# Projection matmuls of an attention and gated-MLP kernel issued as four 32-column tiles

## The chip, the cores and the metric

The kernel runs on one core of a Trainium2 chip. The time is device microseconds of one execution, given as a median over runs; beside it stands one profiled execution, with the span from its first to its last instruction. Engine names: PE is the matrix engine (PEld are its weight loads), DVE the vector engine, ACT the scalar engine, POOL the GpSimd engine, SP the engine that issues most DMAs.

## What is computed

The input x is layer-normalised, and two branches read the result: multi-head attention with 32 heads of 20 columns, and a gated MLP. They are multiplied after a SiLU and added to x.

```python
x = A_x                                   # 1 x 2048 x 640, bf16
xn = _layernorm(x, axis=-1)
# attention: H = 32, Dh = 20
qkv = (xn @ wqkv).reshape(B, S, 3, H, Dh)
scores = einsum("bhqd,bhkd->bhqk", q, k) * Dh ** -0.5
o = einsum("bhqk,bhkd->bhqd", softmax(scores), v)
s = o @ wo
# gated MLP: F = 1728
h = sigmoid(xn @ w_gate) * (xn @ w_up)
g = silu(h @ w_down)
return x + s * g
```

## The kernel before

**Stages.** A first stage normalises 16 token tiles of 128 rows, transposes them into `xnT` (128 model rows x 5 slices x 2048 tokens, in four chunks of 512 tokens), and computes K, the first Q and part of V for the first four heads. Then the main stage runs 32 blocks: 8 groups of four heads (`GH`) times 4 chunks of 512 queries (`QC`). A last stage finishes the final block's output rows.

**The score path.** A score tile is 128 keys x 512 queries of one head. It has a contraction of 32 rows (20 used, one for a bound), so the four heads of a group stand in four row quarters of the PE array: `score_mm` (L859-861) uses `tile_position=(32*j, 0)`. The array form is "rows". A round writes up to two score tiles into one of two double banks `scA`, and up to two more into the three single banks `bk` (`bank`).

**Two engines take exponentials.** ACT reads `scA` (a pair at once), sometimes with a third tile in a `bk` (L1171, L1172), and writes `pt`. DVE takes other tiles from a `bk` by integer steps: an `iv` pass per tile (L1194) and three passes over four tiles (L945, L948, L951) that make `pb`. Every score tile goes to one of the two engines: ACT's is one PV matmul, DVE's two.

**The PV path.** `pv_emit` (L887-901) multiplies with V. The stationary operand has 21 columns, and the four heads stand in four column quarters, `tile_position=(0, 32*j)`, all adding into one bank `oacc`. The array form is "columns", four matmuls in a round.

**The projections.** K and Q for the first two groups (`k_mm1` L467, `mk_q` L471), K and Q for units of six heads (120 columns, `u_mm` L503), gate and up for 128 hidden columns each (`mk_gu` L622, `mm` and `mm2`): each is 5 matmuls, one for each slice of the contraction, of a 128 x 128 (or 120) weight against 512 tokens of `xnT`, into one `bk`. `q_bound` (L173) adds one more to a Q. These use the whole array ("none"). V (`mk_v`), the down projection (`mk_down`) and the output projection (`mk_out`) hold tokens stationary and also use the whole array. In the first stage `k_mm` and `q_mm` (L138, L163) do the same work as whole-array matmuls.

**The order.** The order on PE, ACT and DVE is written out by a planner at build time: it steps a clock `now` by 0.02 us, gives each operation a fixed duration, and emits the instruction that it picks. On PE it chooses between a score round ("F"), a PV round ("PV") and the next matmul of a projection item ("M"). `T_F`, `T_PV` and `T_MM` are 0.2133; a step in another `mode` than the one before pays `T_MODE`, 0.107. An item takes a `bk` that is free (`flex`), and releases it when DVE or ACT has read it. DVE claims a score tile in a round if its queue is short and a bank is free (L1283, L1288); what it does not claim goes to ACT. SP's DMAs (gate and up weights, Q and K through DRAM, the softmax divisor) are issued in the order in which the planner reaches them.

Of the kernel before, what the change touches and what calls it, by code (L numbers as in the profile page):

```python
# [18 lines left out]
P = 128  # L19
# [9 lines left out]
UC = UH * DH  # L29
# [20 lines left out]
def kernel(  # L50
# [11 lines left out]
    nc = tc.nc  # L62
# [4 lines left out]
    KD = D // P  # L67
# [30 lines left out]
    xnT = persist.tile([P, NQC, KD, QC], BF16, name="xnT")  # L98
# [13 lines left out]
    mds = [const.tile([P, P], BF16, name=f"md{i}") for i in range(2)]  # L112
# [16 lines left out]
    def wslice(g, t, kd):  # L129
        return wqks[g % 2][:, kd * 2 + t, :, :].rearrange("p j e -> p (j e)")  # L130
# [37 lines left out]
    def q_abs(ps):  # L168
        aq = wk.tile([P, QC], BF16, tag="aq", bufs=4, name="aq")
        nc.scalar.activation(out=aq, in_=ps, func=ACT.Abs)  # L170
        return aq

    def q_bound(ps, g, aq):  # L173
        nc.tensor.matmul(ps, lhsT=mds[g % 2], rhs=aq, start=False, stop=True, skip_group_check=True)

    def q_evac(ps, q):
        nc.vector.tensor_scalar_mul(out=q, in0=ps, scalar1=qscale)
# [218 lines left out]
    wgu_tiles = {}  # L396
# [23 lines left out]
    T_F, T_PV, T_MM, T_MODE = 0.2133, 0.2133, 0.2133, 0.107  # L420
# [44 lines left out]
            ev_at[("md", g)] = t + 0.3  # L465

    def k_mm1(ps, g, c, kd):  # L467
        nc.tensor.matmul(ps, lhsT=wslice(g, 1, kd), rhs=xnT[:, c, kd, :],
                         start=(kd == 0), stop=(kd == KD - 1))

    def mk_q(b, at):  # L471
        g, c = divmod(b, NQC)
        st = {}

        def alloc():
            st["ps"] = misc_ps()

        def mm(kd):
            nc.tensor.matmul(st["ps"], lhsT=wslice(g, 0, kd), rhs=xnT[:, c, kd, :],
                             start=(kd == 0), stop=(kd == KD - 1))  # L480

        def ab():
            st["aq"] = q_abs(st["ps"])

        def ev():
            q_evac(st["ps"], qts[b % 3])
        return Item([("PE", alloc, [(T_MM, lambda kd=kd: mm(kd)) for kd in range(KD)]),
                     ("ACT", 0.48, ab),
                     ("PE", None, [(T_MM, lambda: q_bound(st["ps"], g, st["aq"]))]),
                     ("DVE", 0.60, ev, "free", lambda t: q_at.__setitem__(b, t))], at, pre=[("md", g)])  # L490


    wus, mku = {}, {}
# [7 lines left out]
        wus[u] = w  # L501

    def u_mm(st, u, i, c, kd):  # L503
        nc.tensor.matmul(st["ps"][0:UC, :], lhsT=wus[u][:, kd, i, :], rhs=xnT[:, c, kd, :],  # L504
                         start=(kd == 0), stop=(kd == KD - 1))

    def mk_ku(u, c, at):
        st = {}
# [113 lines left out]
    def mk_gu(c, kf, at):  # L622
# [15 lines left out]

        def mm(key, i, kd):
            w = wgu_tiles[(c, k2)]  # L640
            nc.tensor.matmul(st[key][0:fs, :], lhsT=w[:, i, kd, ko * P:ko * P + fs],  # L641
                             rhs=xnT[:, c, kd, :], start=(kd == 0), stop=(kd == KD - 1))

        def th():
            st["t"] = w2.tile([P, QC], BF16, tag="tnh", bufs=2, name="tnh")
# [4 lines left out]
                                           in1=st["u"][0:fs, :], op0=ALU.add, op1=ALU.mult)  # L650

        def mm2(kd):
            nc.tensor.matmul(st["g"], lhsT=wgu_tiles[(c, k2)][:, 0, kd, P:2 * P],
                             rhs=xnT[:, c, kd, :], start=(kd == 0), stop=(kd == KD - 1))

        def th2():
            st["t"] = w2.tile([P, QC], BF16, tag="tnh", bufs=2, name="tnh")
# [380 lines left out]
    with tc.manual_schedule(engines={ENG.PE, ENG.Activation, ENG.DVE}):  # L1038
# [16 lines left out]
        dve_pass = []  # L1055
        dve_last = None
        cur = None
        mode = None
        blk_loaded = -1
        active = []  # L1060
        u_next, k_next, q_next, k_at = 0, PG, PG * NQC, {}
# [37 lines left out]
        while chain or items or glu_items or any(it.i < len(it.ops) for it in active):  # L1099
# [127 lines left out]
            if free["PE"] <= now and chain and chain[0][0] == "PE" and chain_at <= now:  # L1227
                _, dur, f = chain.pop(0)
                f()
                free["PE"] = now + dur  # L1230
                chain_at = now + dur + PL
                mode = "M"
            if free["PE"] <= now:
                s = slots[nfill % 2]
                s_empty = s["a"] is None
# [43 lines left out]
                if nxt == "F":  # L1279
# [17 lines left out]
                    if jobs or d_new is not None:  # L1297
                        for x, t in enumerate(jobs):
                            score_mm(scA[nfill % 2][:, x, :] if x < 2 else bank[nfill % 2], *t)
                        if d_new is not None:  # L1300
                            score_mm(bank[d_bank], *d_new[2])
                            if len(dcur["jobs"]) == GH:
                                dcur = None
                        end = now + T_F + (T_MODE if mode != "F" else 0.0)
                        if d_new is not None:
                            dq.append((d_new[0], d_new[1], d_bank, end + PL))
                            flex[d_bank] = 1e9
                        if jobs:
                            s["a"], s["at"], s["ends"] = jobs, end + PL, 0.0
                            if len(jobs) == SLOT:  # L1310
                                flex[nfill % 2] = 1e9
                            nfill += 1
                        free["PE"] = end
                        mode = "F"
                    elif pv_ok:
                        nxt = "PV"
                    elif m_ok:
                        nxt = "M"
                if nxt == "M":
# [9 lines left out]
                    op = cur.ops[cur.i]  # L1329
                    if step == 0 and op[1] is not None:  # L1330
                        op[1]()
                    dur = op[2][step][0] + (T_MODE if mode != "M" else 0.0)
                    op[2][step][1]()
                    step += 1
                    free["PE"] = now + dur
# [3 lines left out]
                        finish(cur, now + dur)  # L1339
                        cur = None  # L1340
                elif nxt is None and fill and can_fill(fill[0][0]):
                    free["PE"] = now + fill[0][1] + (T_MODE if mode != "M" else 0.0)
                    fill.pop(0)[2]()
                    mode = "M"
                elif nxt == "PV":
                    dur = T_PV + (T_MODE if mode != "PV" else 0.0)
                    b = pv_block[0]
                    pv_emit(us, now + dur)
                    free["PE"] = now + dur
# [41 lines left out]
```

## Time and profile before

| what | us |
|---|---|
| median of 5 runs (lowest, highest) | 839.89 (839.62, 841.19) |
| the profiled execution | 839.89 |
| its span | 838.2 |
| PE, matmuls | 787.1 busy (94%), 6354 recorded |
| PE, weight loads | 278.8 busy (33%) |
| ACT | 795.7 busy (95%) |
| DVE | 765.0 busy (91%) |
| POOL | 78.1 busy (9%) |
| granted PE clock, mean | 0.996 |

A few per cent of the matmuls may have no record: gate and up stand with 471 matmuls beside 520 weight loads. The end of a matmul is modelled, so its length (0.38 us for 512 columns) is longer than its stream; the distance between starts tells how fast PE goes. Consecutive activations overlap too: a pair of score banks is recorded with 1.156 us, but the next one starts after about 0.90. The busy time of an engine is the union of its records.

The largest groups in the list of costs, with count, busy time and mean length of one: ACT `pt<-scA`, 729, 719.2 us, 1150 ns; DVE `iv<-bk`, 471, 319.6 us, 683 ns; PE scores `scA<-q,kT`, 1448, 282.6 us, 382 ns, and `bk<-q,kT`, 600, 215.3 us, 383 ns; PE `oacc<-pt,v`, 1577, 182.9 us, and `oacc<-pb,v`, 942, 153.0 us, both 382 ns; PE gate and up at L641, 471, 142.6 us, 383 ns; the 120-column Q and K at L504, 160, 49.3 us, 399 ns.

### The profile page before, as it was taken

To read this page: it belongs to the slowest core of one execution; us is meant where nothing else is said; L and a number is where in the kernel's file an instruction comes from. 1 tells how busy PE (TensorE), PEld (TensorE's weight loads), DVE (VectorE), ACT (ScalarE), POOL (GpSimd) and SP (SyncE) were. 2 spreads that over 40 slices of the span, in tenths; PEclk is the share of its full clock that TensorE was granted. 3 is DMA by queue.
4 is the path that set the end of the run, shared out by engine and by line. 5 is a ranking of instruction groups with operands and counts; after the bars stand their busy time and mean duration, and the time that the engine had idled before them with its cause. 6 is when DMAs were issued, how large, how long until landed. Compare 5 with 4: busy or idle time off the path is not lost.

```text
span 838.2 us, 16932 instructions
## 1 busy us (share of the span) xinstructions
PE 787.1 (94%) x6354; PEld 278.8 (33%) x6411; DVE 765.0 (91%) x1194; ACT 795.7 (95%) x1003; POOL 78.1 (9%) x84
## 2 busy tenths in 40 slices
PE   4799999999999999999999999999999999999995
PEld 2432323333333323333333333333333322333342
DVE  7789899998899998999899999999998988999994
ACT  7799999999999999999999999999999999999970
POOL 5000000000000000000000000000000000001333
PEclk9999999999999999999999999999999999999998
DMA  5621211123222132213112222131421223111643
GB/s 154 201 55 50 60 51 48 46 58 80 73 64 61 46 85 69 71 31 93 52 53 62 68 72 74 49 93 43 117 64 46 60 76 79 28 44 56 183 147 105
DMA packets 92979, 62.21 MB, mean 74 GB/s; under 512 B 34648, under 2 KB 86408, under 8 KB 92896
## 3 DMA queue, kind: packets, MB, share of 16 engines
q1 hardware_dynamic: 92608, 60.79, 26.2%
q8 instruction: 50, 0.82, 0.4%
q10 hardware_dynamic: 288, 0.33, 0.1%
q14 instruction: 33, 0.27, 0.1%
HBM read 46.24 MB, written 12.39 MB: 70 GB/s over the span
## 4 chain that ended last, share of the span: by engine, by line
ACT 47%; PE 32%; DVE 12%; issue 6%; DMA 1%; POOL 1%; SPq 0%; POOLq 0%; ACTq 0%; DVEq 0%
ACT pt L80 43%; PE scA L860 10%; PE oacc L897 6%; PE bk L679 5%; DVE iv L1194 5%; PE bk L641 4%; ACT tnh L80 2%; PE bk L765 2%; PE bk L504 2%; DVE pb L945 2%; DVE pb L951 1%; DVE pb L948 1%; PE psk L140 1%; PE bk L860 1%; ACT td L80 1%
## 5 line engine op out<-in xcount | busy, mean ns | idle before, releaser
L80 ACT ACTIVATE pt<-scA 128x1024 bf16<-128x1024 f32 (+1 forms) x729 | 719.2, 1150 | 3.4 <-PE bk L860 1.7
L1194 DVE TENSOR_SCALAR iv<-bk 128x512 int16<-128x512 f32 x471 | 319.6, 683 | 31.8 <-PE bk L860 30.3
L860 PE MATMUL scA<-q,kT 32*128 32x512 bf16 x1448 | 282.6, 382 | 16.7 <-ACT pt L80 9.6
L860 PE MATMUL bk<-q,kT 32*128 32x512 bf16 x600 | 215.3, 383 | 1.1 <-DVE iv L1194 1.0
L897 PE MATMUL oacc<-pt,v 128*21 128x512 bf16 x1577 | 182.9, 382 | 0.6 <-ACT pt L80 0.3
L860 PEld LDWEIGHTS <-kT 32*128 32x128 bf16 x2048 | 89.0, 91 | 261.6 <-issue 247.2
L897 PE MATMUL oacc<-pb,v 128*21 128x512 bf16 x942 | 153.0, 382 | 1.7 <-DVE on L910 1.5
L951 DVE TENSOR_TENSOR pb<-iv,pb 128x2048 bf16<-128x2048 bf16 x118 | 147.4, 1249 | 0.8
L641 PE MATMUL bk<-xnT,wgu 128*128 128x512 bf16 x471 | 142.6, 383 | 3.9 <-issue 1.7
L927 POOL TENSOR_TENSOR on_bf<-on,rl 128x512 bf16<-128x512 f32 x30 | 43.6, 1453 | 692.0 <-DMA rl<-rd 442.5
L80 ACT ACTIVATE pt<-bk 128x512 bf16<-128x512 f32 x129 | 94.2, 730 | 3.9 <-PE bk L860 3.7
L679 PE MATMUL bk<-wd,hT 128*128 128x320 bf16 x448 | 86.9, 302 | 1.2 <-DVE iv L1194 0.7
L945 DVE TENSOR_SCALAR pb<-iv 128x2048 int16<-128x2048 int16 x118 | 85.8, 727 | 2.5
L948 DVE TENSOR_SCALAR pb<-iv 128x2048 int16<-128x2048 int16 x118 | 82.5, 699 | 0.0
L897 PEld LDWEIGHTS <-v 128*21 128x21 bf16 x2519 | 50.4, 90 | 92.0 <-issue 69.4
L641 PEld LDWEIGHTS <-wgu 128*128 128x128 bf16 x520 | 37.2, 97 | 66.2 <-issue 49.9
L679 PEld LDWEIGHTS <-hT 128*128 128x128 bf16 x448 | 34.4, 97 | 46.5 <-issue 37.6
L504 PE MATMUL bk<-xnT,wu 128*120 128x512 bf16 x160 | 49.3, 399 | 0.4 <-DVE iv L1194 0.3
L80 ACT ACTIVATE tnh<-bk 128x512 bf16<-128x512 f32 (+1 forms) x56 | 41.2, 736 | 0.1
L649 DVE SCALAR_TENSOR_TENSOR hT<-tnh,bk 128x512 bf16<-128x512 bf16 x52 | 35.4, 681 | 5.9 <-PE bk L641 5.2
L612 PE MATMUL bk<-wv,xnT 128*128 128x160 bf16 x280 | 29.2, 234 | 0.7 <-ACT pt L80 0.6
L612 PEld LDWEIGHTS <-xnT 128*128 128x128 bf16 x280 | 18.5, 98 | 14.4 <-issue 14.1
(116 smaller groups left out, 381.4 us busy)
## 6 DMA issues: line engine op xcount, KB each, us to landing
wgu<-in_B_w_gate_dram SPq DMA_DIRECT2D x24, 320.0 KB
wgu<-in_B_w_up_dram SPq DMA_DIRECT2D x24, 320.0 KB
rl<-rd SPq DMA_DIRECT2D x120, 64.0 KB
gq_dram<-gqs SPq DMA_DIRECT2D x32, 160.0 KB
xnT<-gq_dram SPq DMA_DIRECT2D x12, 320.0 KB
xt<-in_A_x_dram SPq DMA_DIRECT2D x16, 160.0 KB
wd<-in_B_w_down_dram SPq DMA_DIRECT2D x1, 2080.0 KB
oU<-on_bf SPq DMA_DIRECT2D x104, 20.0 KB
```

The source lines that it names most:

```text
L80: return nc.scalar.add_instruction(mybir.InstActivation(func=func, name=nc.get_next_instruction_name(), engine=ENG.Activation, ins=[nc.sca ...
L504: nc.tensor.matmul(st["ps"][0:UC, :], lhsT=wus[u][:, kd, i, :], rhs=xnT[:, c, kd, :], start=(kd == 0), stop=(kd == KD - 1))
L612: nc.tensor.matmul(st["ps"][:, i * 2 * GC:(i + 1) * 2 * GC], lhsT=xn_tok(tts[i], kd), rhs=wvs[pr][:, kd, :], start=(kd == 0), stop=(kd == ...
L641: nc.tensor.matmul(st[key][0:fs, :], lhsT=w[:, i, kd, ko * P:ko * P + fs], rhs=xnT[:, c, kd, :], start=(kd == 0), stop=(kd == KD - 1))
L679: nc.tensor.matmul(st["ps"][:, 0:HD], lhsT=hT[0:fsz[kf], kf, t4 * P:(t4 + 1) * P], rhs=wd[0:fsz[kf], kf, h * HD:(h + 1) * HD], start=(kf = ...
L860: nc.tensor.matmul(dst, lhsT=kTs[(b // NQC) % 2][32 * j:32 * j + 32, kt * P:(kt + 1) * P], rhs=qts[b % 3][32 * j:32 * j + 32, :], start=Tr ...
L897: nc.tensor.matmul(oacc[32 * j:32 * j + DH + 1, :], lhsT=lhsT, rhs=u["src"], start=first, stop=last, tile_position=(0, 32 * j), skip_group ...
L927: nc.gpsimd.tensor_tensor(out=on_bf, in0=on, in1=rl, op=ALU.mult)
L945: nc.vector.tensor_scalar(out=pb[:, 0, :, :].bitcast(I16), in0=iv, scalar1=0x7F80, scalar2=1, op0=ALU.bitwise_and, op1=ALU.bitwise_or)
L948: nc.vector.tensor_scalar(out=pb[:, 1, :, :].bitcast(I16), in0=iv, scalar1=0x007F, scalar2=0x3F00, op0=ALU.bitwise_and, op1=ALU.bitwise_or)
L951: nc.vector.tensor_tensor(out=pb[:, 1, :, :], in0=iv.bitcast(BF16), in1=pb[:, 1, :, :], op=ALU.mult)
L1194: nc.vector.tensor_scalar(out=d["iv"][:, j, :], in0=bank[bk], scalar1=B_OFF, scalar2=0.0, op0=ALU.add, op1=ALU.max)
```

## The change

Every 512-wide projection of the main stage, and `q_bound`, goes through a new helper `cols`. It splits the weight's columns into pieces of up to 32 and issues one matmul for each, all with the same moving operand, into the partition quarter that belongs to the piece; `tile_position=(0, o)` puts each into a column quarter of the array, as in the PV rounds. A weight of 128 columns gives four matmuls, one of 120 columns three of 32 and one of 24. The last gate/up tile (64 gate and 64 up columns side by side) gives four. V, the down and output projections, and the first stage's `k_mm` and `q_mm` stay whole.

The planner gets a second state, `tiling`, beside `mode`. A step now pays `T_MODE` when its array form differs from the last one's, not when its kind does: a projection (recognised by its duration `T_MM`) and a PV round have the form "columns", V, down and output projections "none", score rounds "rows". A score round still pays by `mode`. Its constants are unchanged.

```diff
+    def cols(ps, w, rhs, start, stop):
+        n = w.shape[1]
+        for o in range(0, n, 32):
+            m = min(32, n - o)
+            nc.tensor.matmul(ps[o:o + m, :], lhsT=w[:, o:o + m], rhs=rhs, start=start, stop=stop,
+                             tile_position=(0, o), skip_group_check=True)
+
     def q_bound(ps, g, aq):
-        nc.tensor.matmul(ps, lhsT=mds[g % 2], rhs=aq, start=False, stop=True, skip_group_check=True)
+        cols(ps, mds[g % 2], aq, False, True)
...
     def k_mm1(ps, g, c, kd):
-        nc.tensor.matmul(ps, lhsT=wslice(g, 1, kd), rhs=xnT[:, c, kd, :],
-                         start=(kd == 0), stop=(kd == KD - 1))
+        cols(ps, wslice(g, 1, kd), xnT[:, c, kd, :], kd == 0, kd == KD - 1)
...
     def u_mm(st, u, i, c, kd):
-        nc.tensor.matmul(st["ps"][0:UC, :], lhsT=wus[u][:, kd, i, :], rhs=xnT[:, c, kd, :],
-                         start=(kd == 0), stop=(kd == KD - 1))
+        cols(st["ps"], wus[u][:, kd, i, :], xnT[:, c, kd, :], kd == 0, kd == KD - 1)
...
         def mm(key, i, kd):
             w = wgu_tiles[(c, k2)]
-            nc.tensor.matmul(st[key][0:fs, :], lhsT=w[:, i, kd, ko * P:ko * P + fs],
-                             rhs=xnT[:, c, kd, :], start=(kd == 0), stop=(kd == KD - 1))
+            cols(st[key], w[:, i, kd, ko * P:ko * P + fs], xnT[:, c, kd, :], kd == 0, kd == KD - 1)
...
                         end = now + T_F + (T_MODE if mode != "F" else 0.0)
+                        tiling = "rows"
...
-                    dur = op[2][step][0] + (T_MODE if mode != "M" else 0.0)
+                    form = "columns" if op[2][step][0] == T_MM else "none"
+                    dur = op[2][step][0] + (T_MODE if tiling != form else 0.0)
+                    tiling = form
...
-                    free["PE"] = now + fill[0][1] + (T_MODE if mode != "M" else 0.0)
+                    free["PE"] = now + fill[0][1] + (T_MODE if tiling != "none" else 0.0)
+                    tiling = "none"
...
-                    dur = T_PV + (T_MODE if mode != "PV" else 0.0)
+                    dur = T_PV + (T_MODE if tiling != "columns" else 0.0)
+                    tiling = "columns"
```

`mk_q`'s `mm` and `mk_gu`'s `mm2` are changed in the same way as `k_mm1`.

## The prediction

> **What bounds the kernel now.** I read the page's busy shares and slices first, then the chain of work that ended last, then the timelines of ScalarE and TensorE, then the order of instructions of both kernels.
>
> ```profile
> PE 787.1 (94%) x6354; PEld 278.8 (33%) x6411; DVE 765.0 (91%) x1194; ACT 795.7 (95%) x1003; POOL 78.1 (9%) x84
> ACT  7799999999999999999999999999999999999970
> ACT 47%; PE 32%; DVE 12%; issue 6%; DMA 1%; POOL 1%; SPq 0%; POOLq 0%; ACTq 0%; DVEq 0%
> ```
>
> Three engines are above 90%, but ACT is full in every slice from the third to the last but one, and it holds 47% of the chain. PE is second with 32%. A busy share hides small waits, so I priced ACT by the distance between starts, from its timeline:
>
> ```profile
> 299.30 0.76 ACT L80 ACTIVATE tnh<-bk 128x512 bf16<-128x512 f32 x1
> 299.78 0.77 ACT L80 ACTIVATE pt<-bk 128x512 bf16<-128x512 f32 x1
> 300.25 4.95 ACT L80 ACTIVATE pt<-scA 128x1024 bf16<-128x1024 f32 x5
> 305.10 0.59 ACT L80 ACTIVATE tnh<-bk 128x512 bf16<-128x512 f32 x1
> 305.58 1.03 ACT L80 ACTIVATE pt<-scA 128x1024 bf16<-128x1024 f32 x1
> ```
>
> Columns: start, length, what. A 512-wide activation lets the next start after 0.48 us (299.30, 299.78, 300.25). A pair of score banks takes 0.904: that is the commonest distance between starts in the whole trace, and the mean is 0.925. The main stage runs from 33.0 us (first score matmul) to 811.1 (end of the last exponential), 778.1 us. ACT's own need in it: 719 pairs x 0.904 = 650.0; 129 + 10 single exponentials, 56 tanh and 7 abs, 202 x 0.478 = 96.6; 32 narrow tanh x 0.318 = 10.2; sum 756.8. So ACT waits only about 21 us in all, nearly always for a score matmul. Those 21 us, and ACT's need, are what a PE change can move.
>
> **What the change costs on PE.** The PV rounds already have the new form; this is one run of them between score rounds, then runs of the present projections:
>
> ```profile
> 74.01 0.39 PE L860 MATMUL scA<-q,kT 32*128 32x512 bf16 x2
> 74.02 0.39 PE L860 MATMUL bk<-q,kT 32*128 32x512 bf16 x1
> 74.34 0.39 PE L897 MATMUL oacc<-pt,v 128*21 128x512 bf16 x1
> ...
> 74.56 0.38 PE L897 MATMUL oacc<-pb,v 128*21 128x512 bf16 x1
> ...
> 74.78 0.59 PE L897 MATMUL oacc<-pt,v 128*21 128x512 bf16 x4
> 75.00 0.38 PE L897 MATMUL oacc<-pb,v 128*21 128x512 bf16 x1
> ...
> 75.53 0.39 PE L860 MATMUL scA<-q,kT 32*128 32x512 bf16 x2
> 75.54 0.38 PE L860 MATMUL bk<-q,kT 32*128 32x512 bf16 x1
> 75.85 0.39 PE L641 MATMUL bk<-xnT,wgu 128*128 128x512 bf16 x1
> ```
>
> ```profile
> 679.74 1.46 PE L641 MATMUL bk<-xnT,wgu 128*128 128x512 bf16 x6
> 681.13 0.39 PE L860 MATMUL scA<-q,kT 32*128 32x512 bf16 x2
> ```
>
> (a) *Streaming.* A round of four column tiles starts every 0.22 us (74.34, 74.56, 74.78, 75.00). Six whole-array projections end 1.46 us after the first starts; less one length of 0.38 that is 5 steps of 0.216. So 762 projection matmuls become 762 rounds of about the same 0.216 us: nothing won, nothing lost, provided four tiles that stream the *same* xnT columns run side by side as four with different columns do. No row shows that; bounds: 0.216 (PV) and four in sequence, 0.86.
>
> (b) *Instructions.* PE issues 17,380 rows instead of 12,811. After a semaphore instruction at 39.62 us had held the PE queue up and the array had nothing left, the next 12 loads and matmuls started within 53 ns, 4 ns each; a round has 8 per 216 ns. Issue has room; I take nothing.
>
> (c) *Weight loads.* One load becomes four.
>
> ```profile
> L897 PEld LDWEIGHTS <-v 128*21 128x21 bf16 x2519 | 50.4, 90 | 92.0 <-issue 69.4
> L641 PEld LDWEIGHTS <-wgu 128*128 128x128 bf16 x520 | 37.2, 97 | 66.2 <-issue 49.9
> L504 PEld LDWEIGHTS <-wu 128*120 128x120 bf16 x160 | 16.6, 131 | 18.9 <-issue 16.3
> ```
>
> A 128-column load takes 97 ns, a 120-column one 131, a 21-column one 90. Loads show only in the first step after a form switch: 226 ns for gate and up, 263 for the 120-column Q and K (59 such steps), 222 for PV. The new loads have 32 columns. By the PV row the first step becomes 222: 59 x 0.041 + 180 x 0.004 = 3.1 us won. By the 120-column row it becomes 263 everywhere: 180 x 0.037 = 6.7 us lost. I take the PV row, since shape and tiles are nearest.
>
> The Trainium skill speaks against this part twice. "TensorEngine Tiling (Array Packing)", Gotcha 2, says that column tiling excludes Fast Weight Load; the 97 against 131 ns above agrees that a full 128-column load has a fast way, and by that rule alone the sum would lean to the 6.7 us loss. "TensorE: Matmul & The Clock Gate", Part 3 (measured speedup), gives 2.38x for three column tiles instead of 3x; by that a round would be an estimated 1.26 x 0.216 = 0.27 us and PE would need some 42 us more. The PV rows at 0.22 contradict it, and I go by the rows.
>
> (d) *Form switches.* From PV to scores (75.22 to 75.53), from scores to projection (75.54 to 75.85) and back (last step 680.82 to 681.13) the next start comes 0.31 us after the last one, 0.10 more than the stream of 0.213. All three forms pay the same, so turning a projection from "none" into "columns" gains only where it touches PV, and loses where it touches down- or V-projections. In the order of instructions the switches of array form go from 1,591 to 1,560: 31 x 0.10 = 3.1 us won. PE in sum: 3.1 + 3.1 = 6.2 us less (bounds: 6.2 less, 3.6 more).
>
> (e) *What the changed order does.* The planner replans everything. It moves 5 of 2,048 score tiles from DVE (471 to 466, each 0.60 us of iv and about 0.59 us of passes, so 6 us of DVE) to ACT: 725 pairs instead of 719, 4 single activations on scA instead of 10, 128 on bk instead of 129. ACT's need: +6 x 0.904 - 7 x 0.478 = +2.1 us. The scA singles sit in starved places (mean distance 0.857), so with their waits the same edit is worth 6 x 0.925 - 6 x 0.857 - 0.48 = -0.1; I keep both ends and take +2.1.
>
> (f) *ACT's waits.* I added up PE's rows between one score round and the next by the prices above. The sum falls from 712 to 709 us; stretches over 1.5 us, which no activation slot covers (a triple is 0.904 + 0.478 = 1.38), fall from 28 to 14, and the time above 1.38 from 14.1 to 9.7 us. I take these 4.4 us as the fall of ACT's 21 us of waits. Bounds: nothing (the score queue two slots deep covers them), and the whole 6.2 of PE.
>
> (g) *Tail.* After the last exponential 27 us remain. The last slot becomes a triple (+0.48), 40 out-projection matmuls instead of 44 follow the last PV (4 x 0.17 = -0.7), and more stand before it (+5 x 0.17). Sum +0.6, bounds -0.7 to +1.3; the fetches of x and gq at the end may hide all of it, so I take 0. DMAs issued by SP are the same but for the merging of neighbours, and I cost them at nothing: the gate/up loads of 320 KB are fetched one double tile ahead.
>
> Sum: +2.1 - 4.4 + 0 = -2.3 us. The profiled execution took 839.9 (span 838.2 and 1.7 around it) and is itself the median, so 837.6. Own range, from -0.1 - 6.2 to +2.1 - 1: 833.5 to 841.
>
> **Rivals.**
>
> *Cover (841.5).* PE's saving falls where ACT never waited: PE itself sat waiting for ACT (9.6 us at the score matmuls, 40 times), so relief only lengthens those waits. ACT then carries its +2.1 with perhaps 0.5 of relief. For it: ACT is full. Against: 32% of the chain is PE's.
>
> *Slower: ACT starves in the new order (845).* All iv, projection and out work shares three banks with the third score of a slot; a late bank release makes a score round start late, and ACT stops. DVE's iv reads already waited 30.3 us for score matmuls. If the replanned order puts waits on ACT's path so that its mean loss per pair rises from 21 ns to 25 or more, over 725 pairs that is +3, with +2.1 a loss of 5. It decides once waits rise by a seventh instead of falling by a fifth. Part (c) at its bad end leads to the same place. Against: the shorter stretches of (f).
>
> *Tiles of one stream do not run side by side.* Each round would cost up to 0.86: 762 x 0.64 = 490 us on PE, a time near 1300. That is also the case of the change not doing what it says. Nothing in PV supports it.
>
> *More gained (833).* All 6.2 us of PE reach ACT and the starved singles vanish too.
>
> **How the numbers follow.** What a measurement of this kernel tells from no change is about 0.2%, 1.7 us. Forecast 0.40 (0.30 faster, 0.10 same); more gained 0.10; cover 0.24 (0.10 same, 0.14 slower); starved 0.24; tiles in sequence 0.02. That makes faster 0.40, same 0.20, slower 0.40. The range reaches from more gained to beyond the starved case: 831 to 848; without tail cases the forecast's own is 833.5 to 841.
>
> **What would show it.** Projection rounds starting every 0.216 us with four starts some 3 ns apart confirm (a); a first step of 222 to 230 ns confirms (c), 260 refutes it. ACT's main stage should need about 759 us and wait about 17; a stage longer than 778 with waits above 21 makes the starved rival right. If ACT's waits stay at 21, cover was right. I am wrong on PE if rounds cost over 0.23 us, and wrong on the end if the stretch after the last exponential leaves 27 us by more than 1.

## The result, and the profile after

| | before | after |
|---|---|---|
| median, us (lowest, highest) | 841.00 (838.99, 845.19) | 844.57 (840.06, 847.58) |
| ratio, with its 95% interval | | 1.0034 [1.0025, 1.0042] |
| span of the profiled execution | 838.2 | 841.3 |
| main stage: first score matmul to last exponential | 33.0 to 811.1 = 778.1 | 33.4 to 814.5 = 781.1 |
| ACT's need in it, by 0.904, 0.478 and 0.318 us | 756.7 | 758.8 |
| ACT's waits in it | 21.4 | 22.3 |
| what is left after it | 27.1 | 26.7 |

The changed kernel is slower, by about 2.9 us by the ratio; the two medians, of 63 and 37 runs, lie 3.6 us apart. The kernel before was run again beside each experiment, so its median here is that of more runs than in the table before the prediction. Two runs of one kernel below (b105_whole), more than 1.5% above its fastest, are left out of its ratio and of its time at equal clock.

The page of the changed kernel, with its busy shares, ACT's and the clock's slices and the chain:

```profile
PE 792.8 (94%) x8692; PEld 282.5 (34%) x8695; DVE 758.6 (90%) x1186; ACT 797.3 (95%) x1002; POOL 78.4 (9%) x84
...
ACT  7699999999999999999999999999999999999970
...
PEclk9899999999999999999999999999999999999998
...
ACT 47%; PE 25%; DVE 17%; issue 7%; DMA 3%; SPq 1%; POOLq 0%; POOL 0%; ACTq 0%; DVEq 0%
```

ACT is as full as before and holds the same 47% of the chain. PE's share has fallen from 32% to 25%, but DVE has risen from 12% to 17% and DMA from 1% to 3%. The clock row has an 8 in its second slice: PE ran at half clock from 33.3 to 40.2 us.

The tiles themselves do what was asked of them. PE's timeline in the changed kernel (start, length, what):

```profile
130.55 0.40 PE L177 MATMUL bk<-xnT,wgu 128*32 128x512 bf16 x4
130.78 0.38 PE L899 MATMUL oacc<-pb,v 128*21 128x512 bf16 x1
...
131.91 1.26 PE L177 MATMUL bk<-xnT,wgu 128*32 128x512 bf16 x20
133.11 0.39 PE L862 MATMUL scA<-q,kT 32*128 32x512 bf16 x2
```

Twenty tiles are five rounds; 1.26 less one length of 0.39 is four steps of 0.218 us. A PV round follows a tiled projection after 0.23 us (130.55 to 130.78), where a change of form took 0.32. The loads, from the groups with shapes kept apart (busy, mean ns, idle before):

```profile
L177 PEld LDWEIGHTS <-wgu 128*32 128x32 bf16 x2160 | 44.9, 95 | 64.9 <-issue 45.8
...
L177 PEld LDWEIGHTS <-wu 128*32 128x32 bf16 x480 | 12.5, 94 | 19.8 <-issue 15.7
...
L177 PEld LDWEIGHTS <-wu 128*24 128x24 bf16 x160 | 10.7, 90 | 0.1
```

The 131 ns of the 120-column load are gone; the loads of these projections now take 90 to 95.

What got worse stands in two other groups, those of DVE's score pass and of its reciprocal of the row sums. In the kernel before, and in the changed kernel:

```profile
L1194 DVE TENSOR_SCALAR iv<-bk 128x512 int16<-128x512 f32 x471 | 319.6, 683 | 31.8 <-PE bk L860 30.3
...
L920 DVE RECIPROCAL rt<-lt 128x16 f32<-128x16 f32 x30 | 7.4, 247 | 1.7 <-DMA lt<-ld 1.7
```

```profile
L1196 DVE TENSOR_SCALAR iv<-bk 128x512 int16<-128x512 f32 x466 | 316.5, 684 | 41.9 <-PE bk L862 40.8
...
L922 DVE RECIPROCAL rt<-lt 128x16 f32<-128x16 f32 x30 | 7.4, 246 | 3.9 <-DMA lt<-ld 3.9
```

DVE waits for score matmuls 40.8 us instead of 30.3, and for the load of `lt` 3.9 instead of 1.7. The first costs nothing, as order_only will show; the second, by the experiments at the end, goes with most of the loss. `lt` is the row sums of a block: `on`, copied from PSUM, goes through DRAM (`ld`, `lt`), DVE takes the reciprocal (`rt`), that goes through DRAM again (`rd`, `rl`), GpSimd multiplies (`on_bf`), and `oU` stores the result.

### The profile page after: what moved, and what is told of

Its sections match the earlier page's. It is cut to its first block, busy times and chain, and to the rows that moved or that the text cites. A ratio compares the mean times of both kernels' runs of the same rounds, so it can differ in the third digit from the quotient of the medians.

```text
span 841.3 us, 21584 instructions
## 1 busy us (share of the span) xinstructions
PE 792.8 (94%) x8692; PEld 282.5 (34%) x8695; DVE 758.6 (90%) x1186; ACT 797.3 (95%) x1002; POOL 78.4 (9%) x84
## 4 chain that ended last, share of the span: by engine, by line
ACT 47%; PE 25%; DVE 17%; issue 7%; DMA 3%; SPq 1%; POOLq 0%; POOL 0%; ACTq 0%; DVEq 0%
ACT pt L80 43%; PE scA L862 7%; DVE iv L1196 6%; PE bk L177 5%; PE oacc L899 5%; PE bk L681 2%; DVE pb L953 2%; ACT tnh L80 2%; PE bk L767 2%; DVE pb L950 2%; DVE pb L947 2%; DMA lt<-ld 1%; ACT td L80 1%; PE psk L140 1%; PE bk L862 1%
## 5 line engine op out<-in xcount | busy, mean ns | idle before, releaser
L80 ACT ACTIVATE pt<-scA 128x1024 bf16<-128x1024 f32 x729 | 722.6, 1165 | 5.0 <-PE bk L862 1.7
L1196 DVE TENSOR_SCALAR iv<-bk 128x512 int16<-128x512 f32 x466 | 316.5, 684 | 41.9 <-PE bk L862 40.8
L177 PE MATMUL bk<-xnT,wgu 128*32 128x512 bf16 x2160 | 157.0, 383 | 1.3 <-DVE hT L652 0.6
L899 PE MATMUL oacc<-pb,v 128*21 128x512 bf16 x932 | 149.3, 382 | 1.5 <-DVE on L912 0.8
L953 DVE TENSOR_TENSOR pb<-iv,pb 128x2048 bf16<-128x2048 bf16 (+1 forms) x117 | 143.6, 1228 | 0.9
L947 DVE TENSOR_SCALAR pb<-iv 128x2048 int16<-128x2048 int16 (+1 forms) x117 | 84.5, 722 | 2.5
L950 DVE TENSOR_SCALAR pb<-iv 128x2048 int16<-128x2048 int16 (+1 forms) x117 | 84.1, 719 | 0.0
L177 PEld LDWEIGHTS <-wgu 128*32 128x32 bf16 x2160 | 44.9, 95 | 64.9 <-issue 45.8
L177 PE MATMUL bk<-xnT,wu 128*32 128x512 bf16 (+1 forms) x640 | 48.6, 383 | 0.4 <-DVE iv L1196 0.2
L616 PE MATMUL bk<-wv,xnT 128*128 128x160 bf16 x280 | 30.3, 243 | 0.6 <-ACT pt L80 0.4
```

Source lines behind the costliest of these rows:

```text
L80: return nc.scalar.add_instruction(mybir.InstActivation(func=func, name=nc.get_next_instruction_name(), engine=ENG.Activation, ins=[nc.sca ...
L177: nc.tensor.matmul(ps[o:o + m, :], lhsT=w[:, o:o + m], rhs=rhs, start=start, stop=stop, tile_position=(0, o), skip_group_check=True)
L616: nc.tensor.matmul(st["ps"][:, i * 2 * GC:(i + 1) * 2 * GC], lhsT=xn_tok(tts[i], kd), rhs=wvs[pr][:, kd, :], start=(kd == 0), stop=(kd == ...
L899: nc.tensor.matmul(oacc[32 * j:32 * j + DH + 1, :], lhsT=lhsT, rhs=u["src"], start=first, stop=last, tile_position=(0, 32 * j), skip_group ...
L947: nc.vector.tensor_scalar(out=pb[:, 0, :, :].bitcast(I16), in0=iv, scalar1=0x7F80, scalar2=1, op0=ALU.bitwise_and, op1=ALU.bitwise_or)
L950: nc.vector.tensor_scalar(out=pb[:, 1, :, :].bitcast(I16), in0=iv, scalar1=0x007F, scalar2=0x3F00, op0=ALU.bitwise_and, op1=ALU.bitwise_or)
```

## How the runs are compared

Each run lists the mean clock granted to PE. Within every kernel the time falls with it: over some 350 runs one slope fits, 0.51 us less for each 0.001 of clock, with 1.07 us left over as scatter. "At 0.995" below is a kernel's time at that clock by this slope; for 12 runs it is good to about 0.6 us. The runs of the kernel before beside the five groups of experiments stand at 841.4, 841.3, 840.9, 841.4 and 841.8 there, so a comparison across groups carries up to another 0.5 us or so. A ratio is against the runs of the kernel before that stand beside the experiment; their medians are in the first row. The last column is DVE's wait for `lt` in the one profiled execution.

| kernel | projections | median, us | ratio [95%] | at 0.995 | wait for lt |
|---|---|---|---|---|---|
| before | whole | 841.0 to 842.8 | 1 | 841.3 | 1.7 |
| changed kernel | tiles | 844.57 | 1.0034 [1.0025, 1.0042] | 843.2 | 3.9 |
| order_only | whole | 840.83 | 0.9992 [0.9977, 1.0008] | 840.5 | 1.7 |
| tiles_only | tiles | 844.04 | 1.0023 [1.0010, 1.0036] | 842.2 | 1.7 |
| tiles_spb | tiles | 843.11 | 1.0013 [0.9999, 1.0028] | 842.7 | 2.6 |
| before_spt | whole | 840.33 | 0.9988 [0.9974, 1.0001] | 840.3 | 0.7 |
| after_spo | tiles | 844.25 | 1.0017 [1.0001, 1.0034] | 842.8 | 4.5 |
| order_spa | whole | 843.00 | 1.0004 [0.9991, 1.0017] | 842.1 | 2.6 |
| dose_attn | 29% tiles | 841.98 | 1.0000 [0.9986, 1.0013] | 840.8 | 0 |
| dose_glu | 71% tiles | 841.16 | 0.9996 [0.9982, 1.0009] | 840.8 | 1.1 |
| best_whole | whole | 844.41 | 1.0028 [1.0013, 1.0044] | 841.1 | 0 |
| best_tiles | tiles | 841.84 | 0.9998 [0.9986, 1.0010] | 839.9 | 0 |
| b105_whole | whole | 846.26 | 1.0064 [1.0035, 1.0093] | 841.9 | 1.5 |
| b105_tiles | tiles | 845.91 | 1.0073 [1.0044, 1.0101] | 840.2 | 0 |
| after_lt | tiles | 843.95 | 1.0031 [1.0013, 1.0049] | 843.0 | none on DVE |
| before_lt | whole | 843.50 | 1.0021 [1.0007, 1.0034] | 841.5 | none on DVE |
| after_lt28 | tiles | 841.85 | 1.0001 [0.9980, 1.0022] | 841.6 | 0 |
| before_free | whole | 841.24 | 0.9980 [0.9964, 0.9996] | 841.1 | 0 |

before_sp and after_sp, at 900 and 917 us, are left out of it. The two b105 kernels ran at clocks of 0.985 and 0.981, so their times at 0.995 are drawn far out and good to about 1 us.

## Experiments: the order, or the tiles?

**order_only** keeps the changed kernel's planner, and so its order, and takes the tiles out of the helper.

```diff
     def cols(ps, w, rhs, start, stop):
-        n = w.shape[1]
-        for o in range(0, n, 32):
-            m = min(32, n - o)
-            nc.tensor.matmul(ps[o:o + m, :], lhsT=w[:, o:o + m], rhs=rhs, start=start, stop=stop,
-                             tile_position=(0, o), skip_group_check=True)
+        nc.tensor.matmul(ps[0:w.shape[1], :], lhsT=w, rhs=rhs, start=start, stop=stop, skip_group_check=True)
```

> The changed kernel's planner and its order on PE, ACT and DVE, instruction for instruction, but every projection again as one whole-array matmul. Three theories. Order: the loss of the changed kernel (0.34%, 2.9 us over before) is in the replanned order, which gives ACT 2.1 us more work and frees none of its waits; the form itself only helps, so without it this is at least as slow as the changed kernel: 844 to 848 us, with about 5 us more of form switches on PE (54 places where PV and projection touch, 0.10 each). Form: column tiles cost time on the chip; then this falls back to before, 840 to 842. SP queue: the builder orders SP's DMAs by its own estimates, which count a tiled projection as four matmuls; here these estimates are the old ones, so the divisor loads come in time (DVE's reciprocal waits 1 to 2 us in all instead of 3.9) and the time is 841 to 843.

**tiles_only** is the kernel before with `cols` and its calls, the planner untouched.

> The kernel before, its planner untouched, so the same order on PE, ACT and DVE, but every projection of the main stage as four 32-column tiles. Order theory: faster than before or the same, 838 to 841 us, since PE loses some 4 us of switches and first steps and ACT has no more to do; waits of ACT below 21 us. Form theory: slower, 843 to 846, with projection rounds above 0.23 us or first steps near 0.26. SP queue theory: 842 to 845, with PE's rounds and switches no dearer, but DVE waiting for the divisor loads more than the 1.7 us of before, because SP's queue stands in another order.

order_only came out at 0.9992 [0.9977, 1.0008] and tiles_only at 1.0023 [1.0010, 1.0036]. The new order costs nothing, though it has all of DVE's longer waits for score matmuls and all of ACT's 2.1 us of added need:

```profile
L1192 DVE TENSOR_SCALAR iv<-bk 128x512 int16<-128x512 f32 x466 | 316.2, 683 | 42.4 <-PE bk L858 41.7
...
L918 DVE RECIPROCAL rt<-lt 128x16 f32<-128x16 f32 x30 | 7.3, 245 | 1.8 <-DMA lt<-ld 1.7
```

These are order_only's groups: 41.7 us of waits for score matmuls, as in the changed kernel, but 1.7 for `lt`. So the loss came with the tiles. But these two pairs differ in more than the tiles. Only PE, ACT and DVE follow the planner; SP's queue is put in order by the builder, which sees four matmuls for a tiled projection. Its 720 DMAs stand in another order at 23 places between order_only and the changed kernel, and at 42 between the kernel before and tiles_only, each moved by at most 5 places.

**before_sp and after_sp** put SP under the planner too, so that its DMAs go in the order in which the program reaches them.

```diff
-    with tc.manual_schedule(engines={ENG.PE, ENG.Activation, ENG.DVE}):
+    with tc.manual_schedule(engines={ENG.PE, ENG.Activation, ENG.DVE, ENG.SP}):
```

> The kernel before, with SP also kept in the planner's own order in the main stage, so that the builder no longer orders SP's DMAs. PE, ACT and DVE stand as before. It is the reference for the next run. A DMA that waits now holds up all that the planner issued after it, so some 0 to 20 us more than before: 841 to 861. Order and form theories say nothing of it; the SP queue theory says that SP's order alone moves the time by more than 1 us, the others that it does not (840 to 842).

> The changed kernel with SP in the planner's own order in the main stage, the same rule as in the run beside it. Order theory: 2 to 4 us slower than that run. Form theory: the same 2 to 4 us. SP queue theory: within 1 us of it, since the rule by which SP is ordered no longer sees the tiles.

They measured 899.55 (1.0696 [1.0671, 1.0722]) and 916.67 (1.0886 [1.0840, 1.0932]): ACT's waits went to 80 and 89 us. SP's order alone can move this kernel by 58 us. Under this rule the changed kernel is again the dearer one, but the two differ in the order of PE, ACT and DVE as well as in the tiles. They are too far from the kernels in question to tell more.

## Experiments: SP's queue, or the tiles?

The next four pin SP's queue to a given order, with PE, ACT and DVE as they were, so that tiles and queue are told apart in both orders.

```diff
+        sp = [i for i in nc.cur_bb.bb.instructions if i.engine == ENG.SP and type(i).__name__ == "InstDMACopy"]
+        for a, b in zip(SP_ORDER, SP_ORDER[1:]):
+            tc.add_manual_dep(sp[b], sp[a].name, mybir.DependencyInfo(
+                mybir.DependencyClass.NoSync, mybir.DependencyReason.DATA), reason="sp order")
```

> The kernel before with its projections as four tiles, the order of PE, ACT and DVE as before, and SP's 720 DMAs held to the very order that they have in the kernel before (in tiles_only, the same kernel without that, 42 places of SP's queue differ, none by more than 5). Theory Q (SP's queue order carries the loss of the tiles): 841.3 us, ratio 1.000, against 1.0023 of tiles_only. Theory T (the tiles themselves carry it, through the granted clock or the rounds): 844 us, ratio 1.002 to 1.003, and a mean granted clock over the runs of 0.992 as in tiles_only (0.9922) against 0.994 of the kernel before.

> The kernel before, untouched but for SP's queue, which is held to the order of tiles_only. Theory Q: 844 us, ratio 1.0023. Theory T: 841.3 us, ratio 1.000, mean granted clock 0.994.

> The changed kernel with SP's queue held to the order of order_only (23 of 720 places differ). Theory Q: 840.8 us, ratio 0.999, and DVE's waits for the load of lt back from 3.9 us to the 1.7 of order_only, so that ACT's wait of 1.40 us at 222.9 goes. Theory T: 844.2 us, ratio 1.0035, with the wait at 222.9 gone or not.

> order_only (whole-array projections in the changed kernel's order) with SP's queue held to the order of the changed kernel. Theory Q: 844.2 us, ratio 1.0035. Theory T: 840.8 us, ratio 0.999, mean granted clock 0.994.

At equal clock, tiles against whole arrays: 842.7 against 841.3 and 842.2 against 840.3 in the old order, 842.8 against 840.5 and 843.2 against 842.1 in the new one. So +1.4, +1.9, +2.3 and +1.1: the tiles cost in all four pairs, and Q falls as the cause. SP's order by itself goes both ways: 1.0 and 0.5 less with the tiled build's queue in the old order, 1.6 and 0.4 more in the new one. after_spo has the wait for `lt` (4.5 us) that Q would have removed. In the old order the waits for `lt` account for a part only: they differ by 0.9 and 1.0 us within the two pairs, which at the 0.63 us of time for each us of wait found below is 0.6 of the 1.4 and 1.9. The rest of the cost there stays open. The granted clock does not carry it either: its mean over the runs was 0.9927 in the changed kernel and 0.9935 in the kernel before, which at 0.51 us for 0.001 is 0.4 us.

## Experiments: a cost by the round, or by chance?

**dose_attn and dose_glu** tile only a part of the projections in the kernel before, with SP's queue pinned to its own: the attention's (`k_mm1`, `mk_q`, `u_mm`, `q_bound`), or gate and up. **best_whole and best_tiles** are a pair in another order, made with five other constants in the changed kernel's planner; SP's queue in best_tiles is pinned to one order, that of best_whole.

```diff
-URGENT, ROUNDS, HOLD, SLACK, LEAD, LAG, D_LAST, D_LAST_END = 0.25, 4, 0.15, 0.2, 40.0, 0.0, 20, 8
-D_ORD, M_ORD, WAIT3, FALL, M_END = 1, 0, 0.4, 1, 1.5
+URGENT, ROUNDS, HOLD, SLACK, LEAD, LAG, D_LAST, D_LAST_END = 0.25, 5, 0.15, 0.25, 30.0, 0.0, 20, 6
+D_ORD, M_ORD, WAIT3, FALL, M_END = 1, 0, 0.4, 1, 1.7
```

The counts in the first two expectations take a matmul and a load for each round; the rounds are 223, 540 and 763, in the same shares.

> The kernel before, its order and SP's order held, with only the attention's projections (q, k, u and their bounds; 446 of the 1,526 tiled rounds) as four tiles. Over the eight kernels run so far (two orders, two SP queues, whole or tiled) the tiles cost 1.6 us at the same mean granted clock (+1.3, +1.9, +2.2 and +0.9 in the four pairs). Theory R (every tiled round costs a little): 29 per cent of 1.6, so 0.5 us over the kernel before, 841.8 us. Theory C (chance: tiles only shift the phase of DVE, POOL and the DMAs against each other, and each variant lands within about 1 us of the same time): anything from -0.8 to +1.7, not in proportion to the rounds.

> As dose_attn, but only gate and up (1,080 of the 1,526 rounds) as four tiles. Theory R: 71 per cent of 1.6, so 1.1 us over the kernel before, and dose_attn and dose_glu add to the 1.6 of all. Theory C: -0.8 to +1.7 over the kernel before, the two not adding to it.

> Whole-array projections in an order that the planner makes with nine other constants (URGENT and so on), its best of some 320 tried by its own clock: 783.7 us of planned time against 785.4 of the changed kernel's order and 787.5 of the kernel before. If planned time is worth what it says (theory P): 1.7 below order_only, so 839.1 us, ratio 0.997. If the chip's scatter between orders is as large as the planner's differences (theory N): 841.5 +- 1.5.

> The same order and the same SP order as best_whole with four tiles for each projection: a fifth pair for the cost of the tiles, in an order of its own. Theory R: 1.6 us above best_whole (1.0 to 2.2). Theory C: between -0.5 and +2.5 of it. By the prediction's own sum on PE it would be below best_whole.

Theory R falls. The doses cost nothing (1.0000 and 0.9996), where R had 0.5 us for the first, too little to be told from nothing, and 1.1 for the second. And in the third order the tiles are faster: best_tiles 841.84 against best_whole 844.41, 1.2 us less at equal clock. Planned time was no guide either: the order with the lowest plan gave 1.0028. The tiles, then, cost something in some orders and not in others. What best_tiles' profile lacks is DVE's wait for `lt` (best_whole has none either):

```profile
L954 DVE RECIPROCAL rt<-lt 128x16 f32<-128x16 f32 x30 | 7.3, 242 | 0.0
```

## Experiments: DVE's wait for the row sums

In the changed kernel one such wait leads straight to the longest new wait of ACT. The chain of waits in the stretch from 216 to 224 us (start, length, what), and then ACT's timeline there:

```profile
215.96 3.33 DMA ld<-on
...
219.30 1.64 DMA lt<-ld
...
221.03 0.25 DVE rt L922
221.29 0.36 DVE gqs L691
221.64 0.04 issue
221.68 0.37 PE bk L862
222.06 0.51 PE bk L681 x3
222.57 0.32 PE scA L862 x2
```

```profile
218.82 2.95 ACT L80 ACTIVATE pt<-scA 128x1024 bf16<-128x1024 f32 x3
222.93 1.94 ACT L80 ACTIVATE pt<-scA 128x1024 bf16<-128x1024 f32 x2 [1.16 <-PE scA L862]
```

`lt` lands late, DVE stands 1.97 us in front of `rt`, and `gqs`, next in DVE's queue, releases its bank late. PE's score round and down projection wait for that bank, and ACT sits idle 1.16 us, 1.40 by starts against order_only. In order_only the same place runs through, five pairs on end:

```profile
218.58 4.79 ACT L80 ACTIVATE pt<-scA 128x1024 bf16<-128x1024 f32 x5
```

**after_lt and before_lt** take the wait from DVE: GpSimd does `rt`, and DVE a reciprocal of the same size on a constant, so that its work stays. All orders are held.

```diff
-        nc.vector.reciprocal(out=rt, in_=lt)
+        nc.vector.reciprocal(out=rt0, in_=rt1)
+        nc.gpsimd.tensor_tensor(out=rt, in0=lt, in1=rtm, op=ALU.pow)
```

**b105_whole and b105_tiles** are a pair in a fourth order (`T_MODE` 0.105 for 0.107 in the planner of the kernel before).

> The changed kernel, all orders and SP's queue held, but the reciprocal of the row sums (rt from lt) done by GpSimd; in its place DVE does one of the same size on a constant, so that DVE's work stays and only its wait for the load of lt is gone (3.9 us in four waits in the changed kernel; one of them leads to ACT's wait of 1.40 us at 222.9). Theory L (these waits carry the loss of the tiles in this order): 1.4 to 2.9 below the changed kernel at the same clock, so 841.7 to 843.2 us. Theory C (the variants scatter by such events, and one more or less moves the rest): within 1 us of the changed kernel, 843.6 to 845.4, with ACT's waits elsewhere in place of that at 222.9.

> The same edit on the kernel before, where DVE's waits for lt are 1.7 us in two places. Theory L: 0 to 0.8 below the kernel before. Theory C: within 1 us of it, either sign. More than 1 us above: GpSimd's reciprocal itself costs time (the normalisation comes later, or GpSimd stands in DVE's way).

> The kernel before with one planner constant changed, the charge for a change of form from 0.107 to 0.105 us: another order of the same work (DVE 1,180 instructions against 1,194), projections whole. Theory C: 839 to 844.5 us, the band in which the eleven variants with SP ordered by the builder or pinned have been. If the order's planned time decides: within 1 us of the kernel before.

> The same order and SP order as b105_whole with four tiles for each projection: the fourth order in which tiles are set against whole arrays (+1.6, +1.6, -2.1 us at equal clock so far). Theory R (tiles cost by the round): 1 to 2 us above b105_whole. Theory C: anywhere from -2.5 to +2.5 of it. By the prediction's sum on PE: below it.

after_lt stayed at 1.0031, and at 843.0 at equal clock against the changed kernel's 843.2: that is C's forecast, not L's, waits elsewhere included. Its profile shows where L may still hold: against the changed kernel, slot for slot, ACT gained 1.40 us at 220.6. Among smaller steps either way it then lost 1.5 at 795.7 and 0.6 at 799.8. A reciprocal takes GpSimd 3 us, and for the last blocks that is on the path to the output projection. after_lt's waits from 788 to 803 (total, times, longest):

```profile
PE bk L799 <- DMA oU<-on_bf: 1.7, 1, 1.7
...
ACT pt L112 <- PE scA L894: 1.3, 1, 1.3
```

before_lt lost 1.1 and 0.9 at the same places. PE ran at half clock from 797.4 to 800.8 us in after_lt and from 796.0 to 799.4 in before_lt, so the second loss of each may be the clock's. In the fourth order the tiles are again no dearer: 1.7 less at equal clock, and the same within the intervals by the ratios. b105_tiles has no wait for `lt`.

**after_lt28** leaves the reciprocals from block 28 on with DVE; **before_free** does so in the kernel before, and without the reciprocal on a constant.

```diff
+        if b < 28:
+            nc.vector.reciprocal(out=rt0, in_=rt1)
+            nc.gpsimd.tensor_tensor(out=rt, in0=lt, in1=rtm, op=ALU.pow)
+        else:
+            nc.vector.reciprocal(out=rt, in_=lt)
```

> after_lt, but with the reciprocals of the last blocks (from block 28) back on DVE: in after_lt ACT's wait of 1.40 us at 222.9 was gone, and 1.5 and 0.6 us came back at 796 and 800, where the output projection waited for the last normalised rows (PE bk from the DMA of oU, 1.7 us). Theory L: 1.4 us or more below the changed kernel at the same mean clock (843.0 at 0.995), so 841.6 there, and about 842.9 in the median. Theory C: within 1 us of the changed kernel at the same clock, 842.0 to 844.0.

> The kernel before with the reciprocals of blocks 0 to 27 on GpSimd and none in their place on DVE: DVE has 28 x 0.24 = 6.8 us less to do and no wait for lt there. A try for a version that beats both. If ACT's waits that begin at DVE are worth their length: 1 to 2 us below the kernel before, ratio 0.998. Theory C: within 1 us, either sign.

after_lt28 is back at the kernel before: 1.0001 [0.9980, 1.0022], and 841.6 at equal clock against the changed kernel's 843.2, so 1.6 less (give or take 0.7 by the scatter of the runs) where L said 1.4 or more and C at most 1.2. Its ACT runs through the place of the lost slot:

```profile
217.09 4.79 ACT L112 ACTIVATE pt<-scA 128x1024 bf16<-128x1024 f32 x5
```

Slot for slot against the changed kernel it gains 1.39 us there, and 0.55, 0.45 and 0.37 at three later places, and gives 0.7, 0.6 and 0.3 back at 231, 240 and 242. The changed kernel waits for `lt` four times, at 99.0 (0.19 us), 221.0 (1.97), 341.0 (1.21) and 486.6 (0.49). Only at the second does ACT's gain follow at once; the three later gains stand 10 us or more behind any of these waits, and order_only has the third wait too (1.12). So taking the waits away brought back 1.6 of the 1.9 us by which the changed kernel is slower at equal clock, and 1.4 of it can be seen at one of them. That the rest is due to the others is not shown.

before_free came out at 0.9980 [0.9964, 0.9996], but at 841.1 against 841.3 at equal clock: 6.8 us taken off DVE are worth next to nothing here. It is the only version whose interval lies below the kernel before; at equal clock no gain can be claimed for it. best_tiles has the lowest time at equal clock, 839.9, but ran at a lower clock, 0.9914, and so ended at 0.9998.

Over the 14 kernels in which DVE does all of `rt`, the wait for `lt` and the time at 0.995 go together (correlation 0.86, from one profile each): 0.63 us, give or take 0.23, for each us of wait. At equal wait the tiles cost 0.1, give or take 0.7. A correlation over kernels that differ in more than this wait is support, not proof.

## Why lt is late with tiles

This part is read from the traces; no kernel was run to test it. The tiles add 4,578 instructions to PE's stream (763 rounds, each with three more matmuls and three more loads), and instructions are fetched by DMA. The DMA queues of the kernel before, and of the changed kernel:

```profile
q1 hardware_dynamic: 92608, 60.79, 26.2%
q8 instruction: 50, 0.82, 0.4%
```

```profile
q1 hardware_dynamic: 92608, 60.79, 26.1%
q8 instruction: 68, 1.11, 0.6%
```

Columns: packets, MB, share of the 16 DMA engines. 18 more packets of 16 KB are 0.29 MB, and 4,578 instructions divided by 18 are 254 to a packet. Each packet takes 1.1 us (0.88 to 1.67 in the changed kernel). The trace does not name the DMA engine of a packet; that data due on the same engine waits behind it is concluded from times. Here are the records around the broadcast `rl` of the block before the late `lt`, worked out from the packets of the two traces:

```
                                  order_only      changed kernel
last rl issued by SP, end         202.81          203.06
16 KB instruction packet          none near       204.41 to 205.30
last four rl packets, start       204.14 to .22   204.38, 204.41, 205.29, 205.51
last rl packet, end               204.30          205.73
on_bf on GpSimd, start, length    205.29, 1.26    206.82, 1.78
first oU issued                   206.58          208.62
ld issued                         214.39          215.96
lt issued                         217.76          219.30
DVE's wait at rt                  0.56            1.97
```

126 of the 128 packets of `rl` are done by 204.49. The last two start as the instruction packet ends, 0.9 us later. GpSimd starts 1.0 to 1.1 us after the last packet in both kernels, and SP, which issues in order, hands the delay on from `oU` to the next block's `ld` and `lt`:

```profile
208.62 3.78 SPq L937 DMA_DIRECT2D oU<-on_bf  x5
212.53 1.52 SPq L606 DMA_DIRECT2D q<-qD  x3
...
215.96 0.54 SPq L914 DMA_DIRECT2D ld<-on  x1
219.30 0.35 SPq L916 DMA_DIRECT2D lt<-ld  x1
```

`on` was ready at 212.2; its store was issued 3.8 us later, behind the stores and loads ahead of it in SP's queue, where order_only took 2.4 us. DVE meanwhile reaches `rt` at about the same time in both kernels (219.06 and 218.83).

The place repeats in the other kernels of this order. In after_spo an instruction packet runs from 203.38 to 204.34, the last three packets of `rl` start only from 204.33 on, and `ld` is issued 3.8 us after `on`; in after_lt28 it runs from 202.78 to 203.71, two packets start after it, and `ld` again takes 3.8. In order_spa none is near, and `ld` takes 2.0.

Over the same 14 traces the last packet of `rl` ends 1.26 us after its issue where no instruction packet overlaps (314 times), and 1.82 where one does (106 times). Some 30 of 180 broadcasts met one in the six kernels with whole arrays, 58 of 180 in the six with all tiles. The number alone does not give the wait: in b105_tiles 13 of 30 met one, and DVE never waits for `lt`; in order_spa 3 did, and DVE waits 2.6 us. Where the packets fall may be what counts, and may be why every order and every dose answered differently; that is not tested.

The Trainium skill, "Runtime: NRT & Kernel Launch", in the section "Instruction fetch mechanics", says that an engine's sequencer fetches its instructions through a DMA queue of its own, in blocks of 16 KiB or 256 instructions. The rows above agree: 16 KB packets in a queue of kind "instruction", 254 added instructions to each added packet. The same section calls the cost of a new block mostly hidden. In the changed kernel the packet at 204.41 us goes with two data packets that start 0.9 us later than their neighbours.

## Why the prediction was wrong

The order of size was right and the sign wrong: 837.6 was forecast, faster by 2.3 us, and 2.9 us slower was measured. The time lies in the wide range of 831 to 848, but above the forecast's own, which ended at 841.

**(a), (c), (d), PE's own sum: right in kind, too large in size.** Rounds follow at 0.216 us with four starts within some 10 ns, the loads take 90 to 95 ns, and the 263 ns step of Q and K is gone. By the weight loads in the traces the changes of form go from 1,530 to 1,500, where 31 fewer were said; order_only has 1,547. In the new order, from 45 to 800 us, order_only to the changed kernel: 57 changes between projections and PV at 0.22 instead of 0.32 us (-5.6), 278 steps from scores to projections 3 ns shorter (-0.8), 297 from projections to scores 11 ns longer (+3.3), 59 first steps of Q and K some 40 ns shorter (-2.4). That is -5.5 for the tiles in one order. The -6.2 of the prediction was counted from the kernel before, where 30 changes fewer are -3.0 in place of the -5.6; the same sum is then about -2.9 (an estimate from these terms). The 11 ns stood in no term of it. Neither of the two rules that spoke against (c) showed in the rounds.

**(b), instructions: a step that failed.** It counted 4,569 more instructions on PE, priced them at their issue, found room there and took nothing. Issue did have room. What it left out is their fetch: 18 packets of 1.1 us among the DMAs that carry the row sums' round trips. The trace of before lists such packets in its queues, and the prediction did not read that row. By the traces one of them leads to the wait of 1.97 us for `lt` and to the 1.4 us that ACT loses at 222.9. That the waits for `lt` carry most of the loss in this order is what after_lt28 shows (1.6 us of 1.9, give or take 0.7); that the fetch makes `lt` late is read from the traces alone.

**(e): right.** ACT's need rose by the 2.1 us that were worked out. order_only, which has them too, is no slower than the kernel before.

**(f): the other step that failed.** 4.4 us of ACT's waits were to go; ACT waited 22.3 instead of 21.4. Of these 1.6 belong to the half clock at 33 to 43 us, and 1.4 to the wait at 222.9. Outside these two places (43 to 210 and 230 to 810 us) the waits did fall, from 20.4 to 17.8 us by the same prices. But order_only, the same order with whole arrays, stands at 17.7 there. So this fall came with the order, and in these two profiles the 5.5 us that the tiles took off PE took nothing off ACT's waits. Less PE time between score rounds does not help where the round waits for DVE, and DVE for a DMA. In the two orders whose tiled kernel has no wait for `lt`, tiles are 1.2 and 1.7 us below whole arrays at equal clock, so a part of (f) may be there to be had.

**(g): tail right, DMAs wrong.** After the last exponential 26.7 us remain, 27.1 before. But that SP's DMAs are "the same" is not so, nor is what the description of the kernel says of their order: the builder sorts them, and the tiles change 23 places. At equal clock that cost or won up to 1.6 us.

**The rivals.** "ACT starves in the new order" gave 845, nearly the measured time, for a wrong reason: the new order alone measured 0.9992. Its last link was right, a bank released late by DVE, but what was late was a DMA, and not the iv pass. "Cover" (841.5) missed the time, but its mechanism, PE's saving where ACT never waited, is what order_only and the changed kernel show away from the wait at 222.9. Tiles of one stream do run side by side, at 0.216 us a round.

## What to carry to other kernels

A change that multiplies instructions should be priced at their fetch too: read the instruction rows among the DMA queues, and ask which small transfers on a round trip share those engines. An engine that executes in a fixed order and waits for a round trip through DRAM should have something else to do first, or the wait should stand on an engine with nothing behind it. In a schedule this tight, one changed form is judged over several orders, at equal clock: single pairs of the same two forms gave anything from -1.7 to +2.3 us.

## What the runs showed that was not expected

- PE drops to half clock for 3.4, 6.8 or 10.2 us in the middle of a dense stage. In the changed kernel it was 33.3 to 40.2 us, in tiles_only also 214.5 to 217.9, in after_spo 221.8 to 228.6, in order_only 34.9 to 41.8, while the kernel before had none in the main stage in the profile shown. The mean clock explains much of a kernel's scatter between runs, 0.51 us for each 0.001.
- SP's order alone is worth 58 us in the kernel before (before_sp), at a mean granted clock of 0.958 instead of 0.994.
- GpSimd needs 3.1 to 3.2 us for 128x16 powers of -1, where DVE needs 0.25 for the reciprocals. In before_free 28 of them add nothing to the time.
